# Converting the expert weights one slot later, first drains on VectorE, and PSUM turned by hand

## The chip, the cores and the metric

The kernel runs on one core of a Trainium2 chip. The metric is device time in microseconds (us) of one execution. The engines: TensorE runs matmuls (PE in the rows, PEld is its weight load), VectorE is DVE, ScalarE is ACT, GpSimd is POOL, SyncE is SP, which here only issues DMAs.

## The reference

Causal attention over 4 batches and 12 heads, 448 positions, head size 64; its output is laid out as 1792 tokens of 768 and goes through two matmuls with `h * cos(h)` between them:

```python
scores = np.matmul(q, k.transpose(0, 1, 3, 2)) / np.sqrt(64)
scores = np.where(causal_mask, -1000000000.0, scores)
attn = np.exp(scores - np.max(scores, axis=-1, keepdims=True))
attn = attn / (np.sum(attn, axis=-1, keepdims=True) + 1e-09)
x = np.matmul(attn, v).transpose(0, 2, 1, 3).reshape(1792, 768)
h = x @ w_in            # w_in: 768 x 2048, float64
g = h * np.cos(h)
out = (g @ w_out).astype(np.float32)   # w_out: 2048 x 768, float64
```

The weights arrive as float64, two 32-bit words per number.

## The kernel before, in words

**Precision.** Every product of the second half is made from a high and a low part of each factor, as three matmuls (high x high, high x low, low x high). The weights' words are turned on the chip into a float32 and then into the two parts. That conversion takes, for each chunk of 128 of the 2048 hidden columns and each of the two matrices: a load of 768 KB into `st` (SP, lines 91 and 96), three ScalarE stages `mk` (133, 135, 137, called `mask`), three VectorE stages `ct` (143, 147, 151, called `pack`), then `halve`: a ScalarE cast (698) and a GpSimd subtraction (699) into the tile `w`, and stores of `w` to DRAM (157) and, for w_out, of the plain sum `raw_d` (160). `st` has two buffers, and the load of item i+2 is issued on SP right behind `pack` of item i.

**Attention.** 24 pairs of heads pass through a software pipeline written out in order, one pair per turn of 6.95 us. In each turn TensorE computes the scores of a later pair (298, the last rows in 307), transposes q and k of another (271), transposes probabilities (369, 379) and multiplies them with v (393, "AV"). ScalarE and VectorE turn the AV result into the high and low parts of x (409, `finish_hi`; 413, `finish_lo`). The loads of q, k, v for later pairs stand on SP. In between, the weights of the first group (the first two chunks of both matrices) are converted in 12 pieces (`convert_weight`, last VectorE step 126). Some matmuls of the second half's first product are put in at the end of attention as "fillers", with the cosine of their results (`ni` 521, `r` 523 to 528, `gh` 542, `gl` 543).

**Pass one.** Tokens 0 to 1023 as two blocks of 512, eight groups of two chunks: 16 slots, numbered k. A slot is: two sums of 18 matmuls (`m1_sum`, 514 to 516, into `h`), with the cosine of each behind it; and then, for the slot before, four token chunks of 12 matmuls (583) into a pair of PSUM banks `o`, each drained into the sum `acc` by one instruction: ScalarE line 566 in the first group (g = 0), VectorE line 568 afterwards. There are three pairs `o`, so the fourth chunk of a slot must wait for the drain of its first. Slot 0's matmuls are the fillers. A slot also converts two weight items; slot 0 has a larger share. All this is in the order in which it is written (`manual_schedule`).

**Pass two.** Tokens 1024 to 1791 with the weights read back from DRAM (`w_in_d`, `w_out_d`, `raw_d`), the second product by a scheme with seven block products (`m2b`, 640); here the framework's scheduler sets the order.

**PSUM.** Attention has a pool `ps` with four banks `p` (transposes, tail scores, AV) and four `s` (scores, transposed probabilities, the fillers' `h`); the second half opens a pool `psm` with two banks `h` and three pairs `o`. The pools hand out the bank.

Of the kernel before, what the change touches and what calls it, by code (L numbers as in the profile page):

```python
# [15 lines left out]
ALU = mybir.AluOpType  # L16
# [4 lines left out]
def kernel(  # L21
# [52 lines left out]
    edge = keep.tile([P, 2], F32, name="edge")  # L74
    nc.vector.memset(edge[:, 0:1], MAGIC)
    nc.vector.memset(edge[:, 1:2], -MAGIC)

    def x_part(t0, n):
        if t0 < TA:
# [3 lines left out]
    def f32(ap):  # L83
        return ap.bitcast(F32)
# [68 lines left out]
        )  # L153
        yield t

    def spill_halves(d, f, w):
        nc.gpsimd.dma_start(out=d[f], in_=f32(w[:]))

    def spill_raw(f, t):
        nc.gpsimd.dma_start(out=raw_d[f // 2, :, f % 2, :], in_=t)  # L160
# [4 lines left out]

    def attention(filler, ps):
        with (
            tc.tile_pool(name="cst", bufs=1) as cst,  # L170
            tc.tile_pool(name="at", bufs=2) as at,
# [41 lines left out]
            for i in range(3):  # L213
# [5 lines left out]
                    nc.scalar.copy(cst.tile([P, 1], BF16, name="tab"), warm[:, 0:1])  # L219
                elif i == 1:  # L220
                    load_qk(1, nc.scalar)
            wps = ps.tile([P, 512], F32, tag="p", bufs=4, name="wps")

            def keep_warm(n):
                for _ in range(n):
# [31 lines left out]
                nat[i].append(vn)  # L257

            def new_bank():
                return ps.tile([P, 512], F32, tag="p", bufs=4, name="bk")

            def score_bank():
                return ps.tile([P, 512], F32, tag="s", bufs=4, name="sc")

            def transpose_qk(i, which):
                src = nat[i][which]
# [259 lines left out]
        nc.vector.scalar_tensor_tensor(r, r, 1.0, hv, op0=ALU.subtract, op1=ALU.mult)  # L528
        yield r

    def m1(ring, g, t0, n, res, pool, tag, bufs):
        for fi in range(2):
            hv = pool.tile([P, 512], F32, tag=tag, bufs=bufs, name="h")[:, 0:n]
            yield from m1_sum(ring, g, fi, t0, n, hv)
            *_, r = cosine_stages(hv, n)
            if t0 < TA:
                res.append(split(r, *g_tiles(n)))
            else:
                res.append(r)
# [12 lines left out]
    order_b = [(TA, 512), (TA + 512, 256)]  # L552

    def moe(ring, early):
        with (
            tc.tile_pool(name="mo", bufs=1) as mo,
            tc.tile_pool(name="psm", bufs=1, space=bass.MemoryType.PSUM) as psm,
        ):
            acc = mo.tile([P, TA // P, 2, EH], F32, tag="acc", name="acc")

            def out_pair():
                return psm.tile([P, 2, 512], F32, tag="o", bufs=3, name="o")

            def add(g, d, o):
                if g == 0:
                    nc.scalar.activation(d, o, AF.Copy, scale=-1.0)  # L566
                else:
                    nc.vector.tensor_tensor(d, d, o, op=ALU.subtract)  # L568

# [109 lines left out]
            def mask(i):  # L679
                if i < len(todo):  # L680
                    for masks[i] in mask_stages(staged[i], mo):
                        yield

            def pack(i):
                if i < len(todo):
                    for t in pack_stages(staged[i], masks.pop(i), mo):
                        masks[i, 0] = t
                        yield
                    staged.pop(i)
                    fetch(i + 2)  # L690
# [13 lines left out]
            def run(*gens):  # L704
                for x in gens:
                    for _ in x:
                        pass
# [5 lines left out]
            def first_spill():  # L713
                for kind in range(2):
                    for f in range(2):
                        spill_halves((w_in_d, w_out_d)[kind], f, ring[kind, f])
                for f in range(2):
                    t = mo.tile([P, DM], F32, tag="ct1", bufs=3, name="wf")
                    nc.gpsimd.tensor_tensor(t, f32(ring[1, f][:, 0]), f32(ring[1, f][:, 1]), op=ALU.add)
                    spill_raw(f, t)  # L720

            def reload_in(g):
                for f in (2 * g, 2 * g + 1):
# [30 lines left out]
                    pend[0](*pend[1:])  # L754

            def slot(g, t0, n, k, prev, first):
                ia, ib, ic = 2 * k, 2 * k + 1, 2 * k + 2
                gs = []
                if first:
                    run(mask(ia), mask(ib), pack(ia))  # L760
                    halve(ia)
                    run(pack(ib))
                    halve(ib)
                    run(mask(ic))
                    return gs
                hv = [psm.tile([P, 512], F32, tag="h", bufs=2, name="h")[:, 0:n] for _ in range(2)]
                run(m1_sum(ring, g, 0, t0, n, hv[0]), mask(ib), pack(ia))
                c0 = cosine_stages(hv[0], n)
                some(c0)
                some(c0)  # L770
                halve(ia)
                some(c0)
                pb = pack(ib)
                some(pb, 2)
                (r0,) = c0
                run(m1_sum(ring, g, 1, t0, n, hv[1]))
                run(pb)
                c1 = cosine_stages(hv[1], n)
                some(c1)
                gs.append(split(r0, *g_tiles(n)))  # L780
                halve(ib)
                some(c1, 2)
                step = (lambda c: None) if prev is None else (lambda c: m2a_chunk(*prev, c))
                step(0)
                mc = mask(ic)
                some(mc)
                (r1,) = c1
                gs.append(split(r1, *g_tiles(n)))
                step(1)
                run(mc)  # L790
                step(2)
                step(3)
                return gs
# [40 lines left out]
            for g in range(NG):  # L834
                last = g == NG - 1
                for u, (t0, n) in enumerate(order_b):
                    gs = []
                    for _ in m1(ring, g, t0, n, gs, psm, "h", 2):
                        pass
                    if last:  # L840
                        gs = [split(r, *g_tiles(n)) for r in gs]
                    else:
                        ops = factors(n, gs)
                    if u == 0 and not last:
                        reload_in(g + 1)
                    flush()
                    if u == 0 and not last:
                        reload_out(g + 1)
                        if g + 1 < NG - 1:
                            block_sums(g + 1)  # L850
                        if g + 2 < NG - 1:
                            reload_raw(g + 2)
                    if acc5 is None:
                        acc5 = mo.tile([P, 7, 2, EH], F32, tag="acc", name="acc5")
                        acc2 = [
                            a[:, x].rearrange("p (e n) -> p e n", e=2)
                            for a in [
                                wpool.tile([P, 2, DM], F32, tag="w1", bufs=2, name="acc2") for _ in range(2)
                            ]
                            for x in range(2)  # L860
                        ]
                    if last:
                        if n == 512:
                            combine([acc5[:, i] for i in range(7)])
                            rows = [acc5[:, a : a + 2, b] for a in (1, 3) for b in range(2)]
                        else:
                            flat = [None] * 7
                            for two, d in zip(PAIRS, acc2):
                                for j, i in enumerate(two):
                                    flat[i] = d[:, j]  # L870
                            combine(flat)
                            rows = [acc2[1], acc2[2]]
                        ws = [tuple(plain[:, f, v] for v in range(2)) for f in range(2)]
                        pend = (m2a, g, t0, n, gs, ws, rows)
                    else:
                        pend = (m2b, g, t0, n, ops, wo_all[:, g % 2], acc5 if n == 512 else acc2)
# [2 lines left out]
    ring = {}  # L879
    early = []  # L880
    pieces = [((kind, fi), j) for kind in range(2) for fi in range(2) for j in range(PARTS)]
    with tc.tile_pool(name="ps", bufs=1, space=bass.MemoryType.PSUM) as ps, tc.manual_schedule():
        filler = m1(ring, 0, *order_a[0], early, ps, "s", 4)


        loaded = None
        for i in attention(filler, ps):
            if loaded is not None:
                key, j, st, half = loaded
                if key not in ring:  # L890
                    ring[key] = weight_tiles(key[0], wpool)
                convert_weight(st, ring[key], wpool, PARTS, j, (half,))
                loaded = (key, j, st, 1) if half == 0 else None
            if loaded is None and pieces and i >= 0:
                key, j = pieces.pop(0)
                loaded = key, j, [load_weight(*key, wpool, PARTS, j)], 0
        for _ in filler:
            pass
# [31 lines left out]
```

## Time and profile before

| | us |
|---|---|
| median of 3 runs | 667.26 (667.07 to 668.03) |
| profiled execution | 668.0 |
| its span, first to last instruction | 666.2 |
| busy: TensorE | 636.7 |
| busy: VectorE | 465.9 |
| busy: ScalarE | 433.4 |
| busy: GpSimd | 362.7 |

The span is cut by the work: attention until about 185.6, pass one from 189.6 to about 460, pass two to the end. A row of a timeline has the start, the duration, the engine, the line, the operation, its output and input; in brackets stands how long the engine had been idle before it and what released it. Matmuls overlap in the pipeline, so the step from one start to the next says more than the duration. PEclk is the granted clock of TensorE as a share of full speed.

### The profile page before, as it was taken

How to read it: one execution, taken by the hardware profiler on the slowest of the kernel's cores; microseconds unless marked ns; L12 is line 12 of the kernel's file. 1: busy time of each engine (PE TensorE's matmuls, PEld its weight loads, DVE VectorE, ACT ScalarE, POOL GpSimd, SP SyncE). 2: the span in 40 equal slices, each digit the busy share in tenths (PEclk: the TensorE clock that was granted, in tenths of full speed). 3: DMA queues.
4: the chain of work that ended last, by engine and by line, in shares of the span. 5: the costliest groups of instructions: out<-in, count | busy, mean ns of one | idle time of the engine just before them, and what ended most of it. 6: DMA issues, size and time to landing. Idle time of an engine off the chain costs nothing.

```text
span 666.2 us, 11201 instructions
## 1 busy us (share of the span) xinstructions
PE 636.7 (96%) x3772; PEld 545.3 (82%) x3772; DVE 465.9 (70%) x1009; ACT 433.4 (65%) x974; POOL 362.7 (54%) x412
## 2 busy tenths in 40 slices
PE   8999999999974789999999999999999999999997
PEld 6677676776754679999999999999998999999997
DVE  5888888988545448877777777637414757766687
ACT  6989899898655787766666666325465645545431
POOL 3666665665324745454545454715638569667710
PEclk9999999999977899999999999999999999999999
DMA  5555555562036967475757574808616326513203
GB/s 129 124 118 125 121 135 121 123 139 63 1 115 224 382 232 243 185 238 186 238 188 238 189 240 182 325 7 287 262 68 214 125 95 207 167 40 127 95 1 142
DMA packets 101752, 107.29 MB, mean 161 GB/s; under 512 B 70720, under 2 KB 89664, under 8 KB 101696
## 3 DMA queue, kind: packets, MB, share of 16 engines
q1 hardware_dynamic: 93920, 74.67, 37.3%
q0 software_dynamic: 5888, 31.46, 12.5%
q10 hardware_dynamic: 1888, 0.46, 0.3%
q8 instruction: 30, 0.49, 0.3%
q14 instruction: 26, 0.21, 0.1%
HBM read 69.60 MB, written 36.96 MB: 160 GB/s over the span
## 4 chain that ended last, share of the span: by engine, by line
PE 86%; DVE 3%; POOL 3%; ACT 3%; DMA 2%; issue 1%; SPq 0%; DVEq 0%; ACTq 0%; POOLq 0%
PE o L583 20%; PE o L640 11%; PE h L514 11%; PE h L516 11%; PE h L515 11%; PE bk L393 6%; PE sc L298 5%; PE sc L369 5%; PE bk L307 3%; PE bk L271 3%; PE sc L379 2%; DMA st<-in_moe_w_out_dram 1%; DVE ct L147 1%; DMA st<-in_moe_w_in_dram 1%; DMA qn<-in_q_dram 1%
## 5 line engine op out<-in xcount | busy, mean ns | idle before, releaser
L568 DVE TENSOR_TENSOR acc<-acc,o 128x768 f32<-128x768 f32 (+1 forms) x129 | 118.2, 925 | 60.1 <-PE o L640 34.8
L583 PE MATMUL o<-w,gh 128*128 128x384 f32 x512 | 110.9, 338 | 15.9 <-ACT acc L566 15.9
L583 PEld LDWEIGHTS o<-w,gh 128*128 128x128 f32 x512 | 91.8, 190 | 18.1 <-ACT acc L566 16.6
L699 POOL TENSOR_TENSOR w<-ct,w 128x768 fp32r<-128x768 f32 x28 | 60.8, 2172 | 83.2 <-ACT w L698 83.2
L543 POOL TENSOR_TENSOR gl<-r,gh 128x512 fp32r<-128x512 f32 (+1 forms) x57 | 61.4, 1078 | 67.8 <-ACT gh L542 67.6
L347 POOL TENSOR_TENSOR pb<-pb,stat 128x768 f32<-128x768 f32 (+2 forms) x72 | 73.9, 1040 | 42.1 <-ACT T L281 19.6
L521 ACT ACTIVATE ni<-h 128x512 int32<-128x512 f32 (+1 forms) x64 | 34.7, 543 | 79.9 <-PE h L516 79.4
L329 ACT ACTIVATE pb<-pb,stat 128x384 f32<-128x384 f32 (+1 forms) x144 | 72.4, 511 | 15.0 <-DVE stat L315 15.0
L514 PE MATMUL h<-xa,w 128*128 128x512 f32 x192 | 77.3, 403 | 4.0 <-DVE r L528 4.0
L515 PE MATMUL h<-xa,w 128*128 128x512 f32 x192 | 76.9, 401 | 0.0
L516 PE MATMUL h<-xa,w 128*128 128x512 f32 x192 | 76.9, 400 | 0.0
L523 DVE SCALAR_TENSOR_TENSOR r<-ni,h 128x512 f32<-128x512 int32 (+1 forms) x64 | 39.4, 616 | 44.9 <-ACT ni L521 44.4
L514 PE MATMUL h<-xb,w 128*128 128x512 f32 (+1 forms) x192 | 64.9, 338 | 1.4 <-DVE r L528 1.4
L583 PE MATMUL o<-w,gl 128*128 128x384 f32 x256 | 65.4, 336 | 0.0
L515 PE MATMUL h<-xb,w 128*128 128x512 f32 (+1 forms) x192 | 64.9, 338 | 0.0
L516 PE MATMUL h<-xb,w 128*128 128x512 f32 (+1 forms) x192 | 64.9, 338 | 0.0
L315 DVE CUSTOM_DVE_ANT_0 pb<-sc,mask 128x384 f32<-128x384 f32 (+1 forms) x144 | 52.9, 418 | 15.0 <-PE sc L298 15.0
L528 DVE SCALAR_TENSOR_TENSOR r<-r,h 128x512 f32<-128x512 f32 (+1 forms) x64 | 39.4, 617 | 30.8 <-ACT r L526 30.1
L640 PE MATMUL o<-wo_all,gh 128*128 128x384 f32 x196 | 49.9, 337 | 0.0
L542 ACT CAST gh<-r 128x512 fp32r<-128x512 f32 (+1 forms) x57 | 30.4, 533 | 28.5 <-DVE r L528 28.5
L514 PEld LDWEIGHTS h<-xa,w 128*128 128x128 f32 x192 | 36.7, 191 | 12.4 <-issue 4.1
L393 PE MATMUL bk<-pm,vn 128*64 128x448 f32 (+3 forms) x384 | 46.8, 386 | 0.0
(108 smaller groups left out, 1464.5 us busy)
## 6 DMA issues: line engine op xcount, KB each, us to landing
w_in_d<-w POOLq DMA_DIRECT2D x16, 768.0 KB, 3.8
w_out_d<-w POOLq DMA_DIRECT2D x16, 768.0 KB, 5.5
w<-w_in_d SPq DMA_DIRECT2D x16, 768.0 KB, 4.6
st<-in_moe_w_in_dram SPq DMA_DIRECT2D x14, 768.0 KB, 5.9
st<-in_moe_w_out_dram SPq DMA_DIRECT2D x14, 768.0 KB, 4.3
wo_all<-w_out_d SPq DMA_DIRECT2D x21, 384.0 KB, 3.9
raw_d<-ct POOLq DMA_DIRECT2D x14, 384.0 KB, 5.6
wr<-raw_d SPq DMA_DIRECT2D x7, 768.0 KB, 8.5
```

The lines of the kernel that those rows point to most:

```text
L315: nc.vector.tensor_tensor_reduce(out=dst, in0=src, in1=m, scale=-1.0, scalar=3.0e38, op0=ALU.add, op1=ALU.min, accum_out=st[:, 0, n : n + 1],)
L329: nc.scalar.activation(dst, dst, AF.Exp, scale=-1.0, bias=st[:, 0, n : n + 1], accum_out=st[:, 1, n : n + 1],)
L347: nc.gpsimd.tensor_tensor(dst, dst, r.to_broadcast(list(dst.shape)), op=ALU.mult)
L393: nc.tensor.matmul(o[heads(j), kc * P : S], lhsT=vn[:, kc, heads(j)], rhs=pm[:, kc, j, kc * P : S], start=(kc == 0), stop=(kc == NB),)
L514: yield nc.tensor.matmul(hv, lhsT=wh[:, f], rhs=x[:, 0, cc, t], start=(cc == 0), stop=False)
L515: yield nc.tensor.matmul(hv, lhsT=wh[:, f], rhs=x[:, 1, cc, t], start=False, stop=False)
L516: yield nc.tensor.matmul(hv, lhsT=wl[:, f], rhs=x[:, 0, cc, t], start=False, stop=(cc == NCC - 1))
L543: nc.gpsimd.tensor_tensor(lo, r, f32(hi), op=ALU.subtract)
L568: nc.vector.tensor_tensor(d, d, o, op=ALU.subtract)
L583: nc.tensor.matmul(o[:, e, 0:EH], lhsT=a[:, cs], rhs=w[:, e * EH : (e + 1) * EH], start=(x == 0), stop=(x == 5),)
L640: nc.tensor.matmul(o, lhsT=ops[i][u][:, b * P : (b + 1) * P], rhs=wo[:, i, v, :], start=(x == 0), stop=(x == 2),)
L699: nc.gpsimd.tensor_tensor(w[:, 1], tf, f32(w[:, 0]), op=ALU.subtract)
```

## The change

1. A slot k converts the items 2k-2, 2k-1, 2k instead of 2k, 2k+1, 2k+2: slot 0 converts nothing, slot 1 starts with an extra `mask` of its first item.
2. The drains of the first group go to VectorE (`tensor_scalar`, times -1).
3. The two PSUM pools become one tile of eight banks, and the places are handed out by counters: `p` 0 to 3, `s` 4 to 7, `h` 4 and 5, pairs `o` at 6, 0 and 2. The fillers' `h` takes `p` places.
4. The four stores of the first group's weights go on SP's queue instead of GpSimd's. The sums `wf` (line 719) that restored the first group's w_out for `raw_d`, and their stores, are gone; instead each of the six w_out pieces of attention stores its float32 `ct` to `raw_d` from SP when it has been converted.

```diff
+    psum = ctx.enter_context(tc.tile_pool(name="ps", bufs=1, space=bass.MemoryType.PSUM))
+    banks8 = psum.tile([P, 8, 512], F32, name="banks")
+    turn = {}
+    def bank(tag, *places):
+        i = turn.get(tag, 0)
+        turn[tag] = i + 1
+        return places[i % len(places)]
+    def new_bank():
+        return banks8[:, bank("p", 0, 1, 2, 3)]
+    def score_bank():
+        return banks8[:, bank("s", 4, 5, 6, 7)]
...
             def out_pair():
-                return psm.tile([P, 2, 512], F32, tag="o", bufs=3, name="o")
+                b = bank("o", 6, 0, 2)
+                return banks8[:, b : b + 2]
+            def h_bank():
+                return banks8[:, bank("h", 4, 5)]
             def add(g, d, o):
                 if g == 0:
-                    nc.scalar.activation(d, o, AF.Copy, scale=-1.0)
+                    nc.vector.tensor_scalar(d, o, -1.0, None, op0=ALU.mult)
...
             def first_spill():
-                        spill_halves((w_in_d, w_out_d)[kind], f, ring[kind, f])
-                for f in range(2):
-                    t = mo.tile([P, DM], F32, tag="ct1", bufs=3, name="wf")
-                    nc.gpsimd.tensor_tensor(t, f32(ring[1, f][:, 0]), f32(ring[1, f][:, 1]), op=ALU.add)
-                    spill_raw(f, t)
+                        spill_halves((w_in_d, w_out_d)[kind], f, ring[kind, f], nc.sync)
...
             def slot(g, t0, n, k, prev, first):
-                ia, ib, ic = 2 * k, 2 * k + 1, 2 * k + 2
+                ia, ib, ic = 2 * k - 2, 2 * k - 1, 2 * k
                 if first:
-                    run(mask(ia), mask(ib), pack(ia))
-                    halve(ia)
-                    run(pack(ib))
-                    halve(ib)
-                    run(mask(ic))
                     return gs
-                run(m1_sum(ring, g, 0, t0, n, hv[0]), mask(ib), pack(ia))
+                run(m1_sum(ring, g, 0, t0, n, hv[0]))
+                if k == 1:
+                    run(mask(ia))
+                run(mask(ib), pack(ia))
...
-        filler = m1(ring, 0, *order_a[0], early, ps, "s", 4)
+        filler = m1(ring, 0, *order_a[0], early, new_bank)
...
-                convert_weight(st, ring[key], wpool, PARTS, j, (half,))
+                tf = convert_weight(st, ring[key], wpool, PARTS, j, (half,))
+                if key[0] == 1 and half == 1:
+                    n = DM // PARTS
+                    nc.sync.dma_start(
+                        out=raw_d[key[1] // 2, :, key[1] % 2, j * n : (j + 1) * n], in_=tf
+                    )
```

In the order below, line numbers of the changed kernel are 9 or 10 higher behind the new PSUM lines, up to 15 ahead of them (133 becomes 148, 521 becomes 530, 566 becomes 576), and every PSUM operand is called `banks`.

ScalarE before, from the second conversion item of slot 0 to slot 1's first cosine (`mk` is a mask stage, L698 the cast of a converted weight, `ni` and `r` the cosine):

```order
L133 ACTIVATE mk<-st,edge 128x768
L135 ACTIVATE mk<-mk,edge 128x768
L137 ACTIVATE mk<-mk 128x768
L698 CAST w_2753<-ct 128x768
L698 CAST w_2763<-ct 128x768
L133 ACTIVATE mk<-st,edge 128x768
L135 ACTIVATE mk<-mk,edge 128x768
L137 ACTIVATE mk<-mk 128x768
L133 ACTIVATE mk<-st,edge 128x768
L135 ACTIVATE mk<-mk,edge 128x768
L137 ACTIVATE mk<-mk 128x768
L521 ACTIVATE ni<-h 128x512
```

ScalarE in the changed kernel, at the same place:

```order
L148 ACTIVATE mk<-st,edge 128x768
L150 ACTIVATE mk<-mk,edge 128x768
L152 ACTIVATE mk<-mk 128x768
L530 ACTIVATE ni<-banks 128x512
L708 CAST w_2487<-ct 128x768
L534 ACTIVATE r<-r 128x512
L535 ACTIVATE r<-r 128x512
L530 ACTIVATE ni<-banks 128x512
L551 CAST gh<-r 128x512
L708 CAST w_2525<-ct 128x768
```

Slot 1's first `ni` now stands behind the first two items' masks; the masks of two further items and two casts that stood ahead of it have moved behind.

VectorE in the changed kernel, slot 1 (L158 to L166 are `pack`, L532 and L537 the cosine, L576 the drains of the first group):

```order
L158 SCALAR_TENSOR_TENSOR ct<-st,mk 128x768
L162 SCALAR_TENSOR_TENSOR ct<-st,ct 128x768
L166 SCALAR_TENSOR_TENSOR ct<-st,ct 128x768
L532 SCALAR_TENSOR_TENSOR r<-ni,banks 128x512
L158 SCALAR_TENSOR_TENSOR ct<-st,mk 128x768
L162 SCALAR_TENSOR_TENSOR ct<-st,ct 128x768
L537 SCALAR_TENSOR_TENSOR r<-r,banks 128x512
L166 SCALAR_TENSOR_TENSOR ct<-st,ct 128x768
L532 SCALAR_TENSOR_TENSOR r<-ni,banks 128x512
L576 TENSOR_SCALAR acc<-banks 128x768
L537 SCALAR_TENSOR_TENSOR r<-r,banks 128x512
L576 TENSOR_SCALAR acc<-banks 128x768 x3
```

This is the order that the slots of later groups had before, with L568 in the place of L576; the drains were on ScalarE.

SP in the changed kernel, in attention, around one store of raw weights (L899), with a weight load behind it and then the q, k and v of a later pair:

```order
L207 DMA vn_93<-in_v_dram 64x2x64
L899 DMA raw_d<-ct 128x256
L111 DMA st<-in_moe_w_out_dram 128x512
L201 DMA qn_87<-in_q_dram 128x3x64 x2
L201 DMA kn_90<-in_k_dram 128x3x64 x2
L219 DMA qn_87<-in_q_dram 64x64 x2
L207 DMA kn_90<-in_k_dram 64x2x64
```

L899 is new; the rows around it stand as before. It waits for the VectorE step that ends the piece's conversion (L126 before).

## Rows read from the trace of the kernel before

**Rows 1.** Windows: us; busy PE, PEld, DVE, ACT, POOL; PEclk; DMA share; GB/s.

```profile
20.00:170.00 150.00, 149.06 (x1154) 105.79 (x1155) 130.97 (x549) 136.35 (x437) 94.12 (x98) 1.00 0.50 116
189.00:195.00 6.00, 5.39 (x13) 4.27 (x14) 0.96 (x2) 3.77 (x5) 1.28 (x1) 0.50 0.52 173
219.90:222.00 2.10, 2.07 (x6) 2.07 (x7) 0.00 (x0) 2.10 (x4) 1.79 (x4) 0.50 0.89 288
238.00:243.60 5.60, 2.44 (x15) 2.20 (x14) 1.88 (x3) 5.32 (x9) 4.38 (x4) 1.00 0.78 278
243.60:460.00 216.40, 216.40 (x1086) 195.17 (x1086) 159.33 (x172) 139.93 (x199) 106.37 (x88) 1.00 0.58 203
```

**Rows 2.** Waits of TensorE: total us, times, longest us.

```profile
PE o L583 <- ACT acc L566: 15.9, 2, 12.8
PE h L514 <- DVE r L528: 5.4, 2, 4.0
```

**Rows 3.** Timeline of TensorE, the starts of slots and the stalls.

```profile
189.60 0.77 PE L514 MATMUL h<-xa,w 128*128 128x512 f32 x1 [4.02 <-DVE r L528]
...
219.93 1.65 PE L583 MATMUL o<-w,gh 128*128 128x384 f32 x4 [12.79 <-ACT acc L566]
...
223.42 0.39 PE L514 MATMUL h<-xa,w 128*128 128x512 f32 x1
...
241.40 0.97 PE L583 MATMUL o<-w,gh 128*128 128x384 f32 x4 [3.15 <-ACT acc L566]
...
243.60 0.39 PE L514 MATMUL h<-xa,w 128*128 128x512 f32 x1
...
260.34 0.39 PE L514 MATMUL h<-xa,w 128*128 128x512 f32 x1
```

**Rows 4.** Timeline of ScalarE, slots 0, 1 and 3.

```profile
191.20 0.99 ACT L133 ACTIVATE mk<-st,edge 128x768 f32<-128x768 f32 x1 [2.46 <-DMA st<-in_moe_w_in_dram]
...
196.34 0.85 ACT L137 ACTIVATE mk<-mk 128x768 f32<-128x768 f32 x1
...
219.08 0.79 ACT L566 ACTIVATE acc<-o 128x768 f32<-128x768 f32 x1
...
249.19 0.58 ACT L521 ACTIVATE ni<-h 128x512 int32<-128x512 f32 x1
```

**Rows 5.** Timeline of VectorE, the fillers' last step, slot 0 and slot 3.

```profile
188.77 0.69 DVE L528 SCALAR_TENSOR_TENSOR r<-r,h 128x512 f32<-128x512 f32 x1 [1.36 <-ACT r L526]
...
199.34 2.48 DVE L151 SCALAR_TENSOR_TENSOR ct<-st,ct 128x768 uint32<-128x768 uint32 x1
...
255.87 0.94 DVE L568 TENSOR_TENSOR acc<-acc,o 128x768 f32<-128x768 f32 x1
```

**Rows 6.** Groups by line and shape: count, busy us, mean ns, idle before.

```profile
L568 DVE TENSOR_TENSOR acc<-acc,o 128x768 f32<-128x768 f32 x121 | 114.0, 950 | 58.4 <-PE o L640 34.3 <-PE o L583 23.5
...
L566 ACT ACTIVATE acc<-o 128x768 f32<-128x768 f32 x18 | 14.2, 806 | 4.6 <-PE o L640 4.5 <-DMA w<-w_in_d 0.2
```

**Rows 7.** Timeline of VectorE in attention: finishing steps, and one converted piece.

```profile
127.19 0.48 DVE L413 TENSOR_TENSOR xb<-bk,xb 128x320 fp32r<-128x320 f32 x1
...
133.81 0.48 DVE L413 TENSOR_TENSOR xb<-bk,xb 128x320 fp32r<-128x320 f32 x1
...
149.75 0.43 DVE L126 SCALAR_TENSOR_TENSOR ct<-st,ct 128x256 f32<-128x256 f32 x1
```

**Rows 8.** Timeline of TensorE in attention: two AV products, one q transpose.

```profile
127.54 0.97 PE L393 MATMUL bk<-pm,vn 128*64 128x448 f32 x4
...
134.49 0.97 PE L393 MATMUL bk<-pm,vn 128*64 128x448 f32 x4
...
159.57 0.60 PE L271 MATMUL bk<-ident,qn 128*128 128x128 f32 x4
```

**Rows 9.** Timeline of SP: the last issue of a pair's q and k.

```profile
150.63 0.62 SPq L192 DMA_DIRECT2D kn<-in_k_dram  x1
```

**Rows 10.** DMA issues from 140 to 160 us: count, KB each, median us to landing.

```profile
kn<-in_k_dram SPq DMA_DIRECT2D x2, 32.0 KB, 2.2
```

More of the change, by code (lines that the diff above doesn't have):

```diff
@@ L154, in pack_stages, with spill_halves @@
         yield t
-    def spill_halves(d, f, w):
-        nc.gpsimd.dma_start(out=d[f], in_=f32(w[:]))
+    def spill_halves(d, f, w, eng=nc.gpsimd):
+        eng.dma_start(out=d[f], in_=f32(w[:]))
     def spill_raw(f, t):
@@ L162, with attention @@
     PARTS = 3
-    def attention(filler, ps):
+    def attention(filler):
         with (
@@ L221, in attention @@
                     load_qk(1, nc.scalar)
-            wps = ps.tile([P, 512], F32, tag="p", bufs=4, name="wps")
+            wps = new_bank()
             def keep_warm(n):
@@ L257, in load_v @@
                 nat[i].append(vn)
[L261 to L265, printed above, removed]
             def transpose_qk(i, which):
@@ L529, in cosine_stages, with m1 @@
         yield r
-    def m1(ring, g, t0, n, res, pool, tag, bufs):
+    def m1(ring, g, t0, n, res, get):
         for fi in range(2):
-            hv = pool.tile([P, 512], F32, tag=tag, bufs=bufs, name="h")[:, 0:n]
+            hv = get()[:, 0:n]
             yield from m1_sum(ring, g, fi, t0, n, hv)
@@ L554, in moe @@
     def moe(ring, early):
[L555 to L558, printed above, removed]
+        with tc.tile_pool(name="mo", bufs=1) as mo:
             acc = mo.tile([P, TA // P, 2, EH], F32, tag="acc", name="acc")
             def out_pair():
-                return psm.tile([P, 2, 512], F32, tag="o", bufs=3, name="o")
+                b = bank("o", 6, 0, 2)
+                return banks8[:, b : b + 2]
+            def h_bank():
+                return banks8[:, bank("h", 4, 5)]
             def add(g, d, o):
                 if g == 0:
-                    nc.scalar.activation(d, o, AF.Copy, scale=-1.0)
+                    nc.vector.tensor_scalar(d, o, -1.0, None, op0=ALU.mult)
                 else:
@@ L756, in slot @@
             def slot(g, t0, n, k, prev, first):
-                ia, ib, ic = 2 * k, 2 * k + 1, 2 * k + 2
+                ia, ib, ic = 2 * k - 2, 2 * k - 1, 2 * k
                 gs = []
                 if first:
-                    run(mask(ia), mask(ib), pack(ia))
-                    halve(ia)
-                    run(pack(ib))
-                    halve(ib)
-                    run(mask(ic))
-                    return gs
-                hv = [psm.tile([P, 512], F32, tag="h", bufs=2, name="h")[:, 0:n] for _ in range(2)]
-                run(m1_sum(ring, g, 0, t0, n, hv[0]), mask(ib), pack(ia))
+                    return gs
+                hv = [h_bank()[:, 0:n] for _ in range(2)]
+                run(m1_sum(ring, g, 0, t0, n, hv[0]))
+                if k == 1:
+                    run(mask(ia))
+                run(mask(ib), pack(ia))
                 c0 = cosine_stages(hv[0], n)
@@ L837, in moe @@
                     gs = []
-                    for _ in m1(ring, g, t0, n, gs, psm, "h", 2):
+                    for _ in m1(ring, g, t0, n, gs, h_bank):
                         pass
@@ L881 @@
     pieces = [((kind, fi), j) for kind in range(2) for fi in range(2) for j in range(PARTS)]
-    with tc.tile_pool(name="ps", bufs=1, space=bass.MemoryType.PSUM) as ps, tc.manual_schedule():
-        filler = m1(ring, 0, *order_a[0], early, ps, "s", 4)
+    with tc.manual_schedule():
+        filler = m1(ring, 0, *order_a[0], early, new_bank)
         loaded = None
-        for i in attention(filler, ps):
+        for i in attention(filler):
             if loaded is not None:
```

## Prediction, made before the changed kernel was run

> **What bounds the kernel now.** I read the windows first, then the waits of TensorE, then its timeline around each wait, and last the timelines of the engines that it waited for. TensorE sets the pace: 149.06 of 150 us busy inside attention, and 216.40 of 216.40 from slot 3 of pass one on [rows 1]. An engine that gets cheaper in those stretches gives nothing. What is left are a few stalls: 15.9 us behind ScalarE's drain, in two waits, and 5.4 us behind the last cosine step `r`, in two waits, the longest 4.0 [rows 2]. The timeline puts nearly all of it between 185.6 and 243.6, where the second half starts [rows 3]:
>
> - 4.02 us before 189.60. The second PSUM pool opens when the first one is empty, and its last user is the fillers' `r`, which ends at 188.77 + 0.69 = 189.46 [rows 5].
> - 12.79 us before 219.93. The fourth token chunk of slot 1 needs the `o` pair of the first, whose drain on ScalarE starts only at 219.08 [rows 4]: it stands behind the masks and casts of four weight items.
> - 3.15 us before 241.40, the same wait in slot 2.
>
> There is a fourth loss. After 4.02 us of idling the granted clock is 0.50 in 189 to 195, and after 12.79 us it is 0.50 in 219.9 to 222; after 3.15 us it stays at 1.00 [rows 1]. Half clock is the 1.2 GHz level. It cost about half of 5.4 busy us, 2.7, the first time and half of 2.1, 1.0, the second.
>
> **The change part by part.**
>
> *The start of slot 1.* With one PSUM tile there is no handover. The fillers' `h` lies in `p` places and slot 1's `h` in 4 and 5, whose last readers are the copies that the last AV itself needs. So slot 1 starts right behind the last AV: 189.60 - 4.02 = 185.58, and its first matmuls keep the clock.
>
> *Slot 1.* A slot at full clock takes 260.34 - 243.60 = 16.74 us [rows 3]; the chunk behind a wait took 243.60 - 241.40 = 2.2, so the rest, two sums and three chunks, is 14.5 to 14.6. They end at 200.1. The fourth chunk waits for the first drain. On ScalarE the first `ni` now stands behind two items' masks, not four. Those masks can't move: the first one starts at 191.20 when its load lands, and the second item's last mask ends at 196.34 + 0.85 = 197.19 [rows 4], where the first sum is long done. From `ni` to the end of the first drain VectorE has exactly the order that slot 3 already had, with one drain instruction in the place of another. There it takes from 249.19 [rows 4] to 255.87 + 0.94 = 256.81 [rows 5], 7.62 us, a `pack` stage stretched beside GpSimd included; such a stretched stage, 2.48 us, stands also in slot 0 [rows 5]. So the drain ends at 197.19 + 7.62 = 204.8 and the chunk starts at 204.9: a new stall of 4.8 us where 4.0 + 12.8 stood. It ends one chunk later, at 207.1.
>
> *The clock.* A pause of 4.8 us lies above the 4.02 that halved the clock and above the 3.15 that didn't. I expect a drop, priced between the two seen, 1.0 and 2.7; I take 2.0.
>
> The Trainium skill ("TensorE: Matmul & The Clock Gate", section "HAM oscillation — how this bites in real kernels") says that a matmul burst after a long wait starts cold. Both long waits here agree, with 0.50 granted behind each. By that rule the new wait costs clock too, as I take it; without it the time is the first rival's.
>
> *Slot 2.* The drains have moved to VectorE and no converted item of slot 0 is left ahead of them; four stores and two sums that took GpSimd's time in slot 2 are gone. With `ni` behind the masks the first drain comes some 8 us after it, and the chunks need it 14.5 us after the slot's start, so I cost the 3.15 us stall at nothing: it goes. If a weight load were 3 us late it would come back whole. Slot 3 then starts at 207.1 + 16.7 + 2.0 = 225.8 instead of 243.60: a gain of 17.8 us.
>
> *Drains.* 18 drains of 806 ns on ScalarE become VectorE instructions; the nearest row there is the subtraction at 950 [rows 6]. In pass one only one of them stands on the path (already in the 7.62). In pass two some ten add 0.95 x 10 = 9.5 us to VectorE in its first group, where TensorE waits little for it; I take 0.2, between -1.4 (the `r` wait of rows 2 that isn't the 4.0 one disappears) and +4.
>
> The Trainium skill ("VectorE: DVE Perf Modes", section "The perf-mode tier table (the rule you actually need)") allows `tensor_scalar` from PSUM up to twice the rate, and its section "Why PSUM operands drop a tier" takes that back for float32. No row here has the operation. By the table the drain is shorter by some 0.4 us and the sum as much less; by the other section it stays at the subtraction's.
>
> *AV in attention.* This is what the change costs. `new_bank` is called four times in a turn (q, k, tail, AV) and has four places, so each AV writes the place of the AV before and must wait for that one's finishing step. Before it didn't wait for it: at 127.54 an AV starts [rows 8] while the step that began at 127.19 runs until 127.67 [rows 7]. Turns alternate: in the next, the step ends at 133.81 + 0.48 = 134.29 and the AV starts at 134.49 [rows 7, 8], 0.20 later. Of the twenty AVs that have the wait, nine start before the step is over, by 0.01 to 0.13 (the pair shown is the worst). From VectorE's end to TensorE's start took 189.60 - 189.46 = 0.14 [rows 3, 5], from ScalarE's 219.93 - 219.87 = 0.06 [rows 3, 4]. A late turn costs 0.05 on average plus 0.06 to 0.14 plus an uncovered weight load: 0.1 to 0.3. Nine of them at 0.18 are 1.6 us; the bounds are 0 (the turn slips and VectorE makes it good) and 20 x 0.25 = 5.0.
>
> *Raw stores from SP.* Six stores of 128 KB, each in front of a weight load and a pair's q and k. SP now waits there until the conversion ends, 149.75 + 0.43 = 150.18 [rows 7], where the last q and k issue ended at 150.63 + 0.62 = 151.25 [rows 9]. Store, load and the seven issues behind it, at up to 0.62 each [rows 9], take 5 to 5.6 us, to 155.5; the last lands 2.2 later [rows 10], at 157.7. TensorE wants them at 159.57 [rows 8]: 1.9 us to spare, so nothing.
>
> *Sum.* The profiled execution is 668.0, span 666.2, so 1.8 around. 666.2 - 17.8 + 1.6 + 0.2 = 650.2; with 1.8 it is 652.0. The median of the runs lies 0.7 below the profiled one: 651.3.
>
> **Rivals.**
>
> - *The clock stays up in slot 1* (or comes back at once). For it: 3.15 us of idling didn't drop it. Against: 4.02 did. 651.3 - 2.0 = 649.3; with a free AV wait 647.7.
> - *Every AV waits.* For it: the slack of the better turns, 0.20, is hardly over the 0.14 of a semaphore, and a waiting matmul's weights load late too. Against: nothing moves those turns. 651.3 + 5.0 - 1.6 = 654.7.
> - *Pass two gets worse*: the scheduler lays it out anew, with VectorE heavier in the first group. Against: the stretch where the drains fall has idle VectorE. 651.3 - 0.2 + 4 = 655.1.
> - *The stall only moves*: slot 1's `ni` or drain meets a late load, as the one in slot 0 to 1 did, and the fourth chunk waits near the old 12.8. For it: masks still stand ahead of `ni`, and they start on a load. Against: both loads in question had landed before 196.34, when the last mask ran [rows 4]. 651.3 + 8 = 659.3.
> - *Slower than before: SP's queue.* A store on SP that holds the queue far longer than a load's issue makes q and k late, and TensorE idles for all beyond the 1.9 us. There are six, so it decides from (667.3 - 651.3) / 6 = 2.7 us beyond the slack, 4.6 us per store; at 6 us each it is 651.3 + 6 x 4.1 = 675.9. Against: an issue on this queue takes about 0.6 us [rows 9], and the wait in front of the store is for a step that ends early.
>
> **How the numbers follow.** Forecast 0.44, clock 0.21, every AV 0.14, pass two 0.10, stall moved 0.07, slower 0.04. What a measurement can tell from no change is about 0.2%, 1.3 us. All but the last are faster by more; a little is left for a heap of small losses: faster 0.93, within 0.2% 0.03, slower 0.04. The forecast's own range is 649 to 653.5. For 8 in 10: down to 646.0 (clock kept, AV free, the pass-two wait gone), up to 658.0 (all AVs, and most of pass two's 4).
>
> **What would show it.** TensorE should start slot 1 within 0.2 us of the last AV at full clock; have one wait in slot 1 of 4 to 5.5 us, now behind VectorE's drain, with a clock of 0.50 behind it; no wait in slot 2; and a new wait of AV (402) for the finishing step (422) in about every second turn, so that a turn is 7.0 or 7.1 us instead of 6.95. I am wrong if the first cosine of slot 1 comes much later than 197, if attention stretches by over 3 us, or if pass two's stretch changes by over 1.5.

## The result and the profile after

The changed kernel takes 650.3 us (median of four runs, 649.45 to 650.83) against 667.4 (now also of four): ratio 0.9741, 95% interval 0.9725 to 0.9758. Forecast was 651.3. The profiled execution is 650.83, its span 649.1 against 666.2, 17.1 shorter.

TensorE's waits after (total us, times, longest), the counterpart of [rows 2]:

```profile
PE banks L593 <- DVE acc L576: 3.5, 1, 3.5
...
PE banks L593 <- DVE acc L578: 0.8, 2, 0.6
```

Of 15.9 us behind drains and 4.0 behind the fillers' `r`, one wait of 3.5 is left; the 0.6 in the second line is new and lies in slot 14. The timeline, the counterpart of [rows 3]: the last AV, slot 1, the fourth chunk, slots 2 and 3, and that wait in slot 14.

```profile
184.85 1.95 PE L402 MATMUL banks<-pm,vn 128*64 128x448 f32 x16
186.73 0.50 PE L523 MATMUL banks<-xa,w 128*128 128x512 f32 x1
...
205.17 1.65 PE L593 MATMUL banks<-w,gh 128*128 128x384 f32 x4 [3.53 <-DVE acc L576]
...
209.18 0.63 PE L523 MATMUL banks<-xa,w 128*128 128x512 f32 x1
...
226.64 0.39 PE L523 MATMUL banks<-xa,w 128*128 128x512 f32 x1
...
426.25 0.98 PE L593 MATMUL banks<-w,gh 128*128 128x384 f32 x4 [0.64 <-DVE acc L578]
```

Slot 1 starts right behind the last AV. Slot 3 starts at 226.64 instead of 243.60: 16.96 of the 17.1 us. From there to the end it is 422.46 us, before 422.60. That near-equality is two changes that cancel. Slots 3 to 13 take 16.74 us each, but slot 14 takes 17.68: with the shift it still converts two items, which it didn't before, and its fourth chunk waits for a drain. All kernels below with the shift have this wait of 0.64 us; the kernel before and old_slots don't. Pass two, from its first matmul to the end, takes 205.98 us instead of 207.07: its 1.4 us wait for `r` is gone. It is 205.9 to 206.3 us in every kernel below with one PSUM tile.

The chain that ends the wait, ScalarE and VectorE (counterparts of [rows 4, 5]):

```profile
191.63 0.98 ACT L148 ACTIVATE mk<-st,edge 128x768 f32<-128x768 f32 x1 [1.68 <-DMA st<-in_moe_w_in_dram]
...
197.49 0.58 ACT L530 ACTIVATE ni<-banks 128x512 int32<-128x512 f32 x1
```

```profile
204.17 0.94 DVE L576 TENSOR_SCALAR acc<-banks 128x768 f32<-128x768 f32 x1
```

The first mask starts on its load, `ni` follows the masks of two items, and the drain ends at 204.17 + 0.94 = 205.11, which is 7.62 us after `ni` started: the number read from slot 3 of before. The windows show the clock behind the wait (columns as in [rows 1]):

```profile
205.00:209.00 4.00, 3.83 (x12) 3.83 (x13) 2.54 (x4) 3.79 (x6) 3.45 (x3) 0.50 0.95 266
209.00:212.00 3.00, 3.00 (x11) 2.44 (x10) 2.55 (x3) 2.52 (x3) 0.00 (x0) 0.70 1.02 426
```

In attention, finishing steps and AVs (counterparts of [rows 7, 8]), VectorE and then TensorE:

```profile
128.08 0.48 DVE L422 TENSOR_TENSOR xb<-banks,xb 128x320 fp32r<-128x320 f32 x1
...
134.89 0.48 DVE L422 TENSOR_TENSOR xb<-banks,xb 128x320 fp32r<-128x320 f32 x1
```

```profile
121.48 0.60 PE L402 MATMUL banks<-pm,vn 128*64 128x448 f32 x2
...
128.62 0.60 PE L402 MATMUL banks<-pm,vn 128*64 128x448 f32 x2
...
135.57 0.60 PE L402 MATMUL banks<-pm,vn 128*64 128x448 f32 x2
```

An AV now starts at 128.62, just behind the step that ends at 128.56; that turn took 7.14 us. The next step ends at 135.37, 0.20 ahead of its AV, and that turn took 6.95.

### The profile page after: what moved, and what is told of

It is laid out like the page before. It is cut to its first block, busy times and chain, and to the rows that moved or that the text cites. A ratio compares the mean times of both kernels' runs of the same rounds, so it can differ in the third digit from the quotient of the medians.

```text
span 649.1 us, 11239 instructions
## 1 busy us (share of the span) xinstructions
PE 637.0 (98%) x3772; PEld 544.7 (84%) x3772; DVE 485.6 (75%) x1028; ACT 421.1 (65%) x955; POOL 358.1 (55%) x404
## 4 chain that ended last, share of the span: by engine, by line
PE 88%; DVE 5%; ACT 2%; DMA 2%; issue 1%; POOL 1%; SPq 0%; ACTq 0%; DVEq 0%
PE banks L593 21%; PE banks L650 12%; PE banks L523 11%; PE banks L524 11%; PE banks L525 11%; PE banks L402 7%; PE banks L307 5%; PE banks L378 4%; PE banks L316 3%; PE banks L280 3%; PE banks L388 1%; DVE pb L324 1%; DMA qn<-in_q_dram 1%; DVE ct L166 1%; DVE ct L162 1%
## 5 line engine op out<-in xcount | busy, mean ns | idle before, releaser
L578 DVE TENSOR_TENSOR acc<-acc,banks 128x768 f32<-128x768 f32 x129 | 118.1, 924 | 40.0 <-PE banks L593 23.4
L593 PE MATMUL banks<-w,gh 128*128 128x384 f32 x512 | 111.2, 338 | 4.2 <-DVE acc L576 3.5
L593 PEld LDWEIGHTS banks<-w,gh 128*128 128x128 f32 x512 | 91.9, 190 | 6.3 <-DVE acc L576 3.9
L338 ACT ACTIVATE pb<-pb,stat 128x384 f32<-128x384 f32 (+1 forms) x144 | 72.5, 511 | 15.9 <-DVE stat L324 15.9
L532 DVE SCALAR_TENSOR_TENSOR r<-ni,banks 128x512 f32<-128x512 int32 (+1 forms) x64 | 39.3, 615 | 50.4 <-ACT ni L530 35.4
L523 PE MATMUL banks<-xa,w 128*128 128x512 f32 x192 | 76.5, 399 | 0.0
L525 PE MATMUL banks<-xa,w 128*128 128x512 f32 x192 | 76.2, 397 | 0.0
L524 PE MATMUL banks<-xa,w 128*128 128x512 f32 x192 | 76.1, 397 | 0.0
L593 PE MATMUL banks<-w,gl 128*128 128x384 f32 x256 | 65.8, 338 | 0.0
L324 DVE CUSTOM_DVE_ANT_0 pb<-banks,mask 128x384 f32<-128x384 f32 (+1 forms) x144 | 52.9, 417 | 16.2 <-PE banks L307 16.2
L524 PE MATMUL banks<-xb,w 128*128 128x512 f32 (+1 forms) x192 | 65.0, 338 | 0.0
L525 PE MATMUL banks<-xb,w 128*128 128x512 f32 (+1 forms) x192 | 64.9, 338 | 0.0
L523 PE MATMUL banks<-xb,w 128*128 128x512 f32 (+1 forms) x192 | 64.8, 338 | 0.0
L537 DVE SCALAR_TENSOR_TENSOR r<-r,banks 128x512 f32<-128x512 f32 (+1 forms) x64 | 39.3, 614 | 19.2 <-ACT r L535 19.0
L162 DVE SCALAR_TENSOR_TENSOR ct<-st,ct 128x768 uint32<-128x768 uint32 x28 | 48.2, 1722 | 1.0
L650 PE MATMUL banks<-wo_all,gh 128*128 128x384 f32 x196 | 48.2, 338 | 0.4 <-ACT gh L551 0.4
```

The costliest lines, as they stand in the source:

```text
L162: nc.vector.scalar_tensor_tensor(t, lo32, 29, t, op0=ALU.logical_shift_right, op1=ALU.bitwise_or)
L324: nc.vector.tensor_tensor_reduce(out=dst, in0=src, in1=m, scale=-1.0, scalar=3.0e38, op0=ALU.add, op1=ALU.min, accum_out=st[:, 0, n : n + 1],)
L338: nc.scalar.activation(dst, dst, AF.Exp, scale=-1.0, bias=st[:, 0, n : n + 1], accum_out=st[:, 1, n : n + 1],)
L523: yield nc.tensor.matmul(hv, lhsT=wh[:, f], rhs=x[:, 0, cc, t], start=(cc == 0), stop=False)
L524: yield nc.tensor.matmul(hv, lhsT=wh[:, f], rhs=x[:, 1, cc, t], start=False, stop=False)
L525: yield nc.tensor.matmul(hv, lhsT=wl[:, f], rhs=x[:, 0, cc, t], start=False, stop=(cc == NCC - 1))
```

## The experiments

Twelve kernels in three groups, one of them (full_again) the changed kernel once more; each ratio is to the kernel before, run on the same chip. "Slot 3" is its start in the trace, "rest" the time from there to the end of the span; together they say where a difference lies. "Slot 3" is of one execution and holds all that lies ahead: the changed kernel's first AV started at 23.69 in one execution and at 22.75 in the other, so 1 us in this column alone says little.

| | us | ratio (95%) | slot 3 | rest |
|---|---|---|---|---|
| before | 667.4 | 1 | 243.60 | 422.6 |
| changed | 650.3 | 0.9741 (0.9725 to 0.9758) | 226.64 | 422.5 |
| shift_alone | 654.1 | 0.9812 (0.9796 to 0.9828) | 229.47 | 424.2 |
| old_slots | 663.6 | 0.9946 (0.9929 to 0.9962) | 240.21 | 421.5 |
| two_pools | 656.9 | 0.9859 (0.9842 to 0.9875) | 224.25 | 430.3 |
| drains_scalar | 651.8 | 0.9777 (0.9763 to 0.9792) | 228.01 | 422.8 |
| av_swap | 651.9 | 0.9758 (0.9736 to 0.9779) | 227.72 | 422.4 |
| stores_back | 652.1 | 0.9761 (0.9740 to 0.9783) | 227.99 | 422.5 |
| early_drain | 657.7 | 0.9847 (0.9823 to 0.9872) | 222.13 | 434.4 |
| pools_act2 | 650.5 | 0.9740 (0.9718 to 0.9762) | 226.22 | 423.4 |
| full_again | 649.9 | 0.9719 (0.9692 to 0.9746) | 225.95 | 422.4 |
| av_parity | 648.6 | 0.9698 (0.9672 to 0.9723) | 224.58 | 422.3 |
| drain_order | 648.5 | 0.9693 (0.9668 to 0.9718) | 220.15 | 426.6 |
| drain_order_av | 647.2 | 0.9683 (0.9657 to 0.9709) | 219.29 | 425.4 |

**The parts of the change.** First the shift alone, on the kernel before (shift_alone):

```diff
-                ia, ib, ic = 2 * k, 2 * k + 1, 2 * k + 2
+                ia, ib, ic = 2 * k - 2, 2 * k - 1, 2 * k
                 if first:
-                    run(mask(ia), mask(ib), pack(ia))
...
                     return gs
```

> The kernel before with only the weight conversion one slot later. Theory (the late conversion carries the gain, and the PSUM handover only fills time in which the fourth chunk would have waited anyway): slot 1 starts after the 4.0 us handover at about 189.6 at half clock, its two sums and three chunks end at 189.6 + 14.6 + 2.7 = 206.9; the first drain, on ScalarE behind the second cosine, ends near 206.5, so TensorE hardly waits there; slot 2 starts near 209 and may still wait up to 3 us: slot 3 at 226 to 229, 650 to 653 us in all. Rival (every part is needed, the handover and its half clock come on top): some 6.7 us more than the full change, about 657.

It brings 14.1 of the 17.0 us at slot 3, and 12.8 by the medians; its 654.1 us lie 1 above the theory's range and 3 below the rival. Slot 1 starts late at half clock and then doesn't wait at its fourth chunk, as the theory had it. Left is a wait in slot 2, with half clock behind it:

```profile
226.44 0.96 PE L583 MATMUL o<-w,gh 128*128 128x384 f32 x4 [2.77 <-ACT acc L566]
```

Then the reverse, the full change with the old slots (old_slots; slot 0's conversions come back with it, not shown):

```diff
-                ia, ib, ic = 2 * k - 2, 2 * k - 1, 2 * k
+                ia, ib, ic = 2 * k, 2 * k + 1, 2 * k + 2
...
```

> The changed kernel with the conversions in their old slots (slot 0 converts two items and masks a third). Theory: the first cosine of slot 1 stands again behind four items' masks, at about 211, and the first drain ends 7.6 us later, near 218.7 instead of 205.1: 13.5 us more, about 664 us. Rival (PSUM, drains and stores carry half of the gain): 657 or less.

The theory's numbers: the first drain ends 7.58 us behind `ni`, at 219.15 (218.7 expected), and the fourth chunk starts then.

```profile
219.21 1.65 PE L593 MATMUL banks<-w,gh 128*128 128x384 f32 x4 [17.95 <-DVE acc L576]
```

Both runs say the same: some 13 of the 17 us are the later conversion. Alone it brings 12.8, and without it the rest of the change brings 3.3 (663.6 against 666.9 for the kernel before on that chip).

Two PSUM pools in the changed kernel (two_pools, the reverse of part 3):

```diff
-                b = bank("o", 6, 0, 2)
-                return banks8[:, b : b + 2]
+                return psm.tile([P, 2, 512], F32, tag="o", bufs=3, name="o")
...
```

> The changed kernel with the two PSUM pools of before. Theory: slot 1 starts 4 us later at half clock and reaches its fourth chunk at about 207, where it no longer waits for the drain; slot 2 starts near 209 as in the changed kernel; AV doesn't wait for the finishing step, which gives 1 us back: 648.5 to 650.5 us. Rival (the single tile saves its 4.0 us and the 2.7 us of half clock): about 657.

The total is the rival's number, the place is not. Slot 3 starts 2.4 us earlier than in the changed kernel, as the theory wanted (0.6 of them lie ahead of the first AV); pass two then takes 7.8 us more. Two groups of TensorE's waits in the whole run; all of the first and 1.1 us of the second lie in pass two:

```profile
PE o L640 <- ACT gh L542: 5.1, 5, 1.0
...
PE o L583 <- DVE acc L568: 1.7, 2, 1.1
```

Pass two's order is the scheduler's, and here it may have changed because the first group's drains changed engines. So the same kernel with those drains on ScalarE in pass two only (pools_act2):

```diff
             def add(g, d, o):
-                if g == 0:
+                if g == 0 and second:
+                    nc.scalar.activation(d, o, AF.Copy, scale=-1.0)
+                elif g == 0:
                     nc.vector.tensor_scalar(d, o, -1.0, None, op0=ALU.mult)
```

> The run with two PSUM pools, but with the first group's drains in pass two on ScalarE as before (on VectorE in pass one). Theory: there the start of slot 3 came at 224.25, 2.4 us earlier than in the changed kernel, and all was lost in pass two, which the scheduler had laid out in another order because the drains had changed engines; with the old drains it needs 422.6 us from slot 3 again, as before: 648 us. Rival (two pools make pass two slow whatever the drains): 656.

From slot 3 on it is 423.4 us again, and the kernel is as fast as the changed one. TensorE's order in pass two is another one than in two_pools: it alternates between the two products in 125 stretches, as before the change, where two_pools has 87. So the loss needs both, pools and drains on VectorE in pass two: either alone doesn't have it. Which rule of the scheduler turned it, no run shows. Up to slot 3 the single tile takes back in attention and in the wait at the fourth chunk what it gives in slot 1; in pass two it gives 1 us (205.98 against 206.93). The measured 650.5 lies between the theory's 648 and the rival's 656. In this execution slot 1 started 0.6 us later than in two_pools, and the half clock behind its 4.0 us wait cost more: the chunks began 11.1 us after slot 1's start, as they did before, where two_pools had 9.7. No run shows why that one came off lighter.

Drains back on ScalarE (drains_scalar), and then, in a run of its own, the first group's stores and sums back on GpSimd (stores_back):

```diff
-                    nc.vector.tensor_scalar(d, o, -1.0, None, op0=ALU.mult)
+                    nc.scalar.activation(d, o, AF.Copy, scale=-1.0)
```

> The changed kernel with the first group's drains on ScalarE. Theory: slot 1's first drain stands behind the second cosine's sine and square there and ends near 206.5 instead of 205.1, the clock as it is: 1 to 2 us more, about 651.7 us. Rival A (the engine doesn't matter): 650.3. Rival B (ScalarE's masks hold it up as before): over 655.

```diff
-                        spill_halves((w_in_d, w_out_d)[kind], f, ring[kind, f], nc.sync)
+                        spill_halves((w_in_d, w_out_d)[kind], f, ring[kind, f])
+                for f in range(2):
+                    t = mo.tile([P, DM], F32, tag="ct1", bufs=3, name="wf")
+                    nc.gpsimd.tensor_tensor(t, f32(ring[1, f][:, 0]), f32(ring[1, f][:, 1]), op=ALU.add)
+                    spill_raw(f, t)
...
```

> The changed kernel with the first group's stores on GpSimd, the two sums there and no raw stores from attention, as before. Theory: the sums and the wait for a sum's store come back into slot 2, whose fourth chunk waits 2.8 us as in the run with the conversion shift alone: 653 us. Rival (slot 2 has room for them): 650.3.

The drains are worth what was expected: 651.8 us, and slot 2 starts 1.6 us later, 1.3 of them in the chain from `ni` to the end of the first drain (8.90 us against 7.62). On the stores the theory was wrong: slot 2's wait did not come back, only 0.2 us of it (the waits from 212 to 230 in stores_back):

```profile
PE banks L593 <- DVE acc L576: 0.2, 1, 0.2
```

shift_alone, with both old parts, waits 2.77 there; drains_scalar, with the old drains alone, doesn't wait in slot 2, and stores_back, with the old stores alone, hardly. So neither part alone brings the wait back. shift_alone also has the two PSUM pools, and no run has them with one of the old parts, so it isn't shown what that wait needs. Of the 1.4 us that stores_back's span is longer than the changed kernel's, 1.0 lie ahead of slot 2 (it starts at 210.16): the first AV starts 0.3 later, and the first mask 0.65 later behind the issue of its load. Whether the edit has a part in that, no run shows; the intervals overlap.

**The price in attention.** Other places for tail scores and AV (av_swap; the two calls that use `turn_bank` are not shown):

```diff
-        return banks8[:, bank("p", 0, 1, 2, 3)]
+        return banks8[:, bank("p", 0, 1)]
+    def turn_bank():
+        return banks8[:, bank("a", 2, 2, 3, 3)]
...
```

> The changed kernel with other places in attention: transposes take 0 and 1, tail scores and AV take 2, 2, 3, 3 in turn, so that an AV writes the place that its turn's tail mask has read, and no longer waits for the finishing step of the AV before. Theory: the 23 steps from first to last AV took 160.35 us before and 161.16 in the changed kernel; the 0.81 us go: 649.5 us. Rival (the difference is not that wait, or the turns slip anyway): 650.3.

From the first AV to the 21st it gained 1.0 us, and it lost more at the end. The last two AVs shared a place, so the last one was the one AV that waited, and the framework had put seven matmuls of slot 1 ahead of it:

```profile
185.00 0.40 PE L526 MATMUL banks<-xa,w 128*128 128x512 f32 x1
185.32 1.95 PE L405 MATMUL banks<-pm,vn 128*64 128x448 f32 x16
187.20 0.50 PE L527 MATMUL banks<-xa,w 128*128 128x512 f32 x1
```

No TensorE time is lost there. But the first weight load of pass one goes out when attention's buffers are free, here at 187.43 behind this AV, and with it come the masks, `ni` and the drain: the fourth chunk waits 5.8 us instead of 3.5, and the time, 651.9 us, is not the theory's. With places by the pair's parity the last AV is free (av_parity; full_again is beside it):

```diff
+    def turn_bank(i):
+        return banks8[:, 3 - i % 2]
...
```

> The changed kernel with tail and AV of an even pair in place 3, of an odd pair in place 2, transposes in 0 and 1: an AV waits for no finishing step, and neither does the last one, which in the run with 2, 2, 3, 3 stood behind seven matmuls of slot 1. Theory (slot 1's chain is anchored on the last AV, which frees the buffers for the first weight load): the 1.0 us of attention is kept to the end: 649.3 us. Rival (slot 1's wait takes it back): 650.3.

> The changed kernel once more, beside the three that follow, on the same chip: 650.3 us.

From the first AV to the one 21 turns later, in full_again and then in av_parity:

```profile
22.75 0.60 PE L402 MATMUL banks<-pm,vn 128*64 128x448 f32 x2
...
169.58 0.60 PE L402 MATMUL banks<-pm,vn 128*64 128x448 f32 x2
```

```profile
23.65 0.60 PE L405 MATMUL banks<-pm,vn 128*64 128x448 f32 x2
...
169.51 0.97 PE L405 MATMUL banks<-pm,vn 128*64 128x448 f32 x4
```

146.83 against 145.86: the wait costs 0.97 us. The wait in slot 1 is 3.48 us against 3.84 in full_again, so it didn't take the gain back. The medians differ by 1.3 us with overlapping intervals: they agree with the theory, and what shows it is the trace.

**The wait that was left.** The first drain on VectorE stood behind the second item's pack and could go ahead. The first try (early_drain, with the places of av_swap) put it and a whole cosine there:

```diff
+                if k <= 3:
+                    ...
+                    run(m1_sum(ring, g, 1, t0, n, hv[1]))
+                    m2a_chunk(*prev, 0)
+                    run(pack(ib))
+                    halve(ib)
+                    gs.append(split(r0, *g_tiles(n)))
+                    *_, r1 = cosine_stages(hv[1], n)
...
```

> The changed kernel with the attention places of the run before, and with slots 1 to 3 written in another order: the first sum's cosine ahead of the masks, and the first drain ahead of the second item's pack. Theory: the 3.5 us wait in slot 1 goes and with it the half clock behind it, about 2.5, and 0.8 from attention: 643.5 us. Rival A (a weight load is late instead, in slot 2 or 3): 646 to 648. Rival B (the clock falls anyway): 646.

Slot 1's wait went, but the second cosine ended so late that the next slot's second sum waited for its bank, three times, and a drain wait came back at 263.88 (the waits from 200 to 270):

```profile
PE banks L526 <- DVE r L540: 7.4, 3, 3.3
...
PE banks L596 <- DVE acc L581: 3.0, 1, 3.0
```

Neither rival had named that, and at 657.7 us it is the slowest of the reorderings. The second try moves the drain and ends both cosines within their slot (drain_order):

```diff
...
+                    some(c0)
+                    m2a_chunk(*prev, 0)
+                    halve(ia)
+                    some(c0)
+                    pb = pack(ib)
+                    some(pb)
+                    (r0,) = c0
+                    run(pb)
+                    c1 = cosine_stages(hv[1], n)
...
```

> The changed kernel with slots 1 to 3 in another order: the first drain straight behind the first cosine step on VectorE, ahead of the second item's pack; in slots 2 and 3 the first cosine ahead of the masks; both cosines of a slot still end within it, which they did not in the run with the early drain. Theory: the 3.5 us wait goes and with it 2.5 us of half clock: 644.3 to 645.5 us. Rival A (the cosine's end holds up the next slot's sums again): over 650. Rival B (a weight load is late in slot 2 or 3): 646 to 649.

With the places of av_parity as well (drain_order_av):

> Both edits: the order of slots 1 to 3 and the places of even and odd pairs. Theory: their gains add, 643.3 to 644.5 us. Rival: not under 645.

At slot 3 drain_order is 5.8 us ahead of full_again, as expected. 4.1 us of that are gone two slots later: in slot 4, the first in the old order, `ni` stands behind a mask that is still late, and the clock falls again. The start of slot 3, the fourth chunk of slot 4 and slot 5:

```profile
220.15 0.39 PE L523 MATMUL banks<-xa,w 128*128 128x512 f32 x1
...
254.04 1.31 PE L593 MATMUL banks<-w,gh 128*128 128x384 f32 x4 [2.04 <-DVE acc L578]
...
257.71 0.47 PE L523 MATMUL banks<-xa,w 128*128 128x512 f32 x1
```

So the theory's time was missed, and 648.5 us lies in rival B's range. A load was late in slot 3, as it said; its mask waited 2.6 us:

```profile
225.08 0.99 ACT L148 ACTIVATE mk<-st,edge 128x768 f32<-128x768 f32 x1 [2.62 <-DMA st<-in_moe_w_in_dram]
```

TensorE didn't wait in slot 3. It waited in slot 4, where the masks waited for no load and `ni` stood behind them (246.29, with the first sum long done); that the late load is the cause is likely, not shown. Both edits together are the fastest of all, 647.2 against 649.9 for the changed kernel on the same chip. Their theory, 643.3 to 644.5, was wrong and the rival right: drain_order_av loses 3.0 us in slot 4 too, without a fall of the clock. The two ratios' intervals overlap, but five of the six runs of full_again lie above all six of this one: that it is faster is likely, by how much is not shown.

## Why the prediction was right

- *What bounds it*: right. 17.0 of the 17.1 us of span lie ahead of slot 3.
- *Start of slot 1*: right, 186.73 against an AV that ends at 186.80.
- *The new wait*: 3.53 us where 4.8 was expected; it ends at 205.17 against 204.9. The chain of 7.62 us was exact, and not by chance: it is 7.58 to 7.64 us in all eight runs that keep this order. That the masks "can't move" was wrong. Their load goes out when the last AV (186.80) and the fillers' last step on GpSimd (186.93) are over, so it moved with slot 1, which started 1.2 us later than in the sum (0.8 for the AV waits, 0.4 because this execution's first AV was later). That the first mask came only 0.43 us later was luck: it started 4.68 us behind the issue of the load instead of 5.43, and no run shows why. First the issue before, then GpSimd's step and the issue in the changed kernel:

```profile
185.77 1.08 SPq L91 DMA_DIRECT2D st<-in_moe_w_in_dram  x2
```

```profile
185.66 1.27 POOL L552 TENSOR_TENSOR gl<-r,gh 128x512 fp32r<-128x512 f32 x1 [4.97 <-ACT gh L551]
186.95 0.97 SPq L106 DMA_DIRECT2D st<-in_moe_w_in_dram  x2
```

- *Clock*: 2.0 taken; the chunk and slot 2 took 4.01 + 17.46 us, and 2.09 + 16.74 at full clock, so 2.6.
- *Slot 2*: no wait, as costed. Of the reason given, drains and stores and sums together, the runs show less: with either of the two put back the wait stays away, and what the PSUM tile does for it is open.
- *AV in attention*: the mechanism and every second turn are right, the size was 1.6 and measured 0.97 to 1.0 (0.81 from the first AV to the last, as the end of attention got 0.2 shorter). The turn of 7.14 us is 6.95, plus 0.13 by which the AV came ahead of the step's end before, plus 0.06 for the release (128.56 to 128.62): the lower of the two prices used, and nothing for a weight load on top.
- *Raw stores from SP*: nothing, as taken; an issue took 0.33 to 0.40 us there:

```profile
165.43 0.35 SPq L899 DMA_DIRECT2D raw_d<-ct  x1
```

- *Pass two*: +0.2 taken for the drains, -1.1 measured: the 1.4 us wait for `r` disappeared, which the prediction had as its lower bound. Against it stands 0.94 in slot 14, for which the prediction had no term. two_pools shows that this was the least safe term: the same drains cost 7.8 us there, beyond the +4 of the bound.
- *The drain on VectorE*: 953 ns, about the subtraction's 950. Of the two sections of the Trainium skill that the prediction names ("VectorE: DVE Perf Modes"), the second, "Why PSUM operands drop a tier", agrees.

```profile
L576 DVE TENSOR_SCALAR acc<-banks 128x768 f32<-128x768 f32 x18 | 17.1, 953 | 6.5 <-PE banks L650 3.4 <-PE banks L593 2.9
```

- *Rivals*: the clock fell to 0.50, only every second AV waited, and `ni` came at 197.49, so the first, the second and the fourth didn't come.

That the total came within 1.0 us is in part luck: attention's price and the load came out about 0.8 us lower each, pass two 1.3 lower, the clock 0.6, slot 14 0.9 and the first AV 0.4 higher.

## What to carry to other kernels

A wait of one engine is priced by following the in-order queue of the engine that it waits for, and that queue by its first late input; a stretch with the same order gives the chain's length, here within 0.04 us. Then ask what the first late input waits for itself: here a load that moved with attention's end. Work that a stage doesn't need until later belongs behind the instruction that frees the next buffer; but if it is only pushed to a later slot, a wait can come back there, as in slot 4 of drain_order and in slot 14 of every kernel with the shift. When banks are placed by hand, count the calls per turn: four calls on four places tie each user to its own last reader.

## What was not expected of the hardware

How long TensorE had idled does not decide alone whether its clock falls. Before, 3.15 us left it at 1.00 [rows 1], while in shift_alone 2.77 us were followed by 0.66 in 226 to 231; in drain_order 2.04 us were followed by 0.57 in the next 4 us, in drain_order_av 2.05 us by 1.00. The windows of shift_alone, drain_order and drain_order_av (TensorE starts again at 226.44, 254.04 and 253.62):

```profile
226.00:231.00 5.00, 4.57 (x16) 4.28 (x17) 1.14 (x2) 4.97 (x8) 2.93 (x4) 0.66 1.00 376
```

```profile
254.00:258.00 4.00, 3.96 (x13) 3.94 (x14) 2.47 (x4) 3.68 (x5) 3.58 (x4) 0.57 0.99 293
```

```profile
252.00:257.00 5.00, 3.38 (x18) 3.16 (x19) 4.37 (x7) 4.80 (x7) 4.58 (x5) 1.00 0.99 301
```

In shift_alone the first six matmuls behind the wait still took their full-clock time, and the half clock set in behind them. Pricing the clock between two waits seen came out near the size here, 2.6 against 2.0, but the length of the waits gave no reason for it, and the runs do not say what decides it.
